# Later weight conversions in batch 0 and a filler that opens with two sums at once: one change to a fused attention and two-layer MLP kernel

## The chip, the cores and the metric

The kernel runs on one core of one Trainium2 chip. The metric is device time in microseconds, the median over runs; of each kernel one execution is also profiled.

## What is computed

Causal attention with a decay bias, then two MLPs of model width 512 and inner width 2048 over 2304 tokens, all in float32. Cut to what matters:

```python
scores = scale * q @ k.T                       # 4 batches, 8 heads, 576 tokens, head size 64
cum = cumsum(maximum(s, 0))
scores = where(causal, -1e9, scores + minimum(-(cum_i - cum_j), 0))
x = softmax(scores) @ v                        # heads side by side: 2304 x 512
h = x @ w_in;   x = (h * sigmoid(1.702 * h)) @ w_out
h = x @ w2_in;  g = P(h) / (Q(h) + 1e-6);  out = g @ w2_out
```

## The kernel before

**Precision.** Products run on TensorE (PE) from pairs of numbers: a float is split into a rounded high part and a low rest, and three products (high x high, low x high, high x low) make one. A block of weights is brought to that form by a **conversion** (`convert`, line 550): lines 558 and 560 on ScalarE (ACT), 561 to 563 on VectorE (DVE), 565 on GpSimd (POOL), 566 on ACT, 567 on POOL, each over 128 x 512 elements. Its raw block of 512 KB is loaded by SP's queue (`load_raw`, lines 547 and 549) into one of three slots of a staging tile, `stgA`. Ten conversions make the first MLP's inner blocks 0 to 4: five for `w_in`, then five for `w_out`. `emit` issues one; two raw loads are issued ahead of all.

**Attention.** A batch has four pairs of heads, a pair has five units: query blocks t = 0, 1, 4, 2, 3. There are 80 units, 20 in each batch. The loop of `attention` goes over steps j. Step j computes the scores of unit j on PE (line 289); DVE adds the mask and takes the minimum (line 319), ACT makes the exponential with its row sum (line 326), DVE the reciprocal (line 336), POOL the normalization (line 339). Three steps later PE transposes the unit (lines 360, 364, 381) and ACT or DVE copies the transposes out (lines 361, 365, 385, 388). A step after that PE multiplies with V (line 406, output `O`), and after t = 4 and t = 3 the values of the pair go to X: the high part by ACT (line 416), the low part by DVE (line 417). In batch 0 the values are taken as each unit is ready, later once per pair. In between, the next pair's Q and K are turned on PE (line 225) and split by ACT (line 213) and DVE (line 216), and moved to their places by POOL or SP.

**The filler.** From batch 1 on, the first MLP of the batch before is done beside the attention, by a generator, `mlp1_first`, that `fill` takes a piece of at three places of each step, by a credit of 1.65 us a step. First it makes ten sums of twelve products each (line 638, tiles `h`: inner blocks 0 to 4, two token halves), each followed by the activation (lines 649 and 652 on ACT, 650 on DVE, 655 on POOL), then the output blocks (line 662). It is started where unit i = j - 3 has i % 20 == 1, that is at steps 24, 44 and 64. Before step 24 PE has no filler; in the first five steps it runs dummy products.

**What sets the order.** PE's order is the program's. The other engines' order is made by a scheduler that keeps each engine's queue in one fixed order; `behind` (a block of `issue_after`) keeps instructions of a conversion from being placed ahead of a given instruction of the same engine. `CONV_J` lists the steps at whose end a conversion of the first ten is emitted, `AHEAD_J` (35 to 55) those of six more. PSUM has eight banks, which all tiles of this phase share.

Of the kernel before, what the change touches and what calls it, by code (L numbers as in the profile page):

```python
# [31 lines left out]
KD = DM // P  # L32
NF = DF // P
F1 = 5
HB = S // 2
# [16 lines left out]
RUN_ENDS = ((0, 1, 4, 2, 3), (3,), (3,), (3,))  # L52
W2_SLOTS = 7
LEAD = 2
CONV_J = (4, 6, 9, 12, 15, 18, 21, 24, 27, 30)
CONV = [(f, 0) for f in range(F1)] + [(f, 1) for f in range(F1)]
STG = 1536
BT_BUFS, G_BUFS = 9, 9
# [3 lines left out]
class Fused:  # L62
# [328 lines left out]
    def unit_values(self, att, u):  # L391
        nc = self.nc
        b, p, t = u
        pr, st = self.pairs[b, p], self.state.pop(u)
        vn = pr["ld"]["v"]
        R = min(P, S - t * P)
        NC = t + 1
        oc = {0: 0, 1: 128, 4: 256, 2: 0, 3: 128}[t]
        if b not in self.X:
            self.X[b] = self.xpool.tile([P, 2, KD, S], F32R, name=f"x{b}", tag="x", bufs=4)  # L400
        if oc == 0:
            pr["O"] = self.bank("O", f"O{b}_{p}_{t}")
        O = pr["O"]
        for c in range(NC):
            for h in range(2):
                nc.tensor.matmul(  # L406
                    O[64 * h : 64 * h + 64, oc : oc + R],
                    lhsT=vn[:, c, h, :], rhs=st["pt"][h, c],
                    start=(c == 0), stop=(c == NC - 1),
                )  # L410
        if t in (3, 4):
            X = self.X[b]
            runs = ((0, 256, 0), (256, 64, 512)) if t == 4 else ((0, 256, 256),)
            for o, w, x0 in runs:
                xh = X[:, 0, p, x0 : x0 + w]
                nc.scalar.activation(xh, O[:, o : o + w], AF.Copy)
                nc.vector.tensor_tensor(
                    X[:, 1, p, x0 : x0 + w], O[:, o : o + w], xh.bitcast(F32), ALU.subtract
                )

# [12 lines left out]
    def attention(self, att, mlp):  # L433
        units = [(b, p, t) for b in range(NB) for p in range(NP) for t in (0, 1, 4, 2, 3)]
        n = len(units)
        nc = self.nc
# [23 lines left out]
        opened = self.moved  # L460
# [3 lines left out]
        for j in range(n + AHEAD + 1):  # L464
            i, k = j - AHEAD, j - AHEAD - 1
            self.zeros = j < ZEROS
            tr = iter(())
            if j < n:
                b, p, t = units[j]
                idx = j % 5  # L470
                if idx == 0 and units[j][1:] != (NP - 1, 0) or (idx == 0 and b + 1 < NB):
                    nprep = self.prep(att, *divmod(b * NP + p + 1, NP), loads.pop(b * NP + p + 1))
            if i >= 0 and i < n and units[i][0] and i % 20 == 1:
                self.filler = chain(self.filler, self.mlp1_first(mlp, units[i][0] - 1))
                self.cold = False
            q = FILL / 20
            if j < n:
                self.unit_scores(att, units[j], 0)
                if j:
                    next(nprep, None)  # L480
                if j == 2:
                    with self.behind((opened,)):
                        later.pop(0)()
                    with self.behind((self.moved,)):
                        self.raw_ahead()
            self.fill(q / 3, 1 if j else 4)
            if 0 <= i < n:
                tr = self.unit_transpose(att, units[i])
                next(tr, None)
            if j < n:  # L490
                self.unit_scores(att, units[j], 1)
            self.fill(q / 3, j < 4)
            for _ in tr:
                pass
            if j < n and idx == 4:
                for _ in nprep:
                    pass
                g = b * NP + p
                g = {0: 3, 1: 4, 2: NB * NP}.get(g, g + 2)
                if g < NB * NP:  # L500
                    with self.behind((opened,)):
                        loads[g] = self.pair_load(att, *divmod(g, NP))
                    later.append(loads[g]["values"])
            if k >= 0:
                run.append(units[k])
                if units[k][2] in RUN_ENDS[units[k][0]]:
                    for u in run:
                        self.unit_values(att, u)
                    run.clear()
                if units[k][2] == 3 and later:  # L510
                    later.pop(0)()
            self.fill(q / 3, j < 4)
            if j == AHEAD_J[0]:
                self.stg_n, self.stg_k = 0, 2
                buf = self.stg_slot[:, 2 * STG : 2 * STG + 1024].bitcast(F32R)
                buf = buf.rearrange("p (i f) -> p i f", i=2)
                for f in AHEAD_F:
                    for half in range(2):
                        self.task(
                            lambda st, f=f, half=half: self.park(st, buf, 1, f, half), 1, f, half  # L520
                        )
            if j in COEF_J:
                with self.behind((*self.tail, self.moved)):
                    if j == COEF_J[0]:
                        self.coefficients()
                    else:
                        self.nc.scalar.activation(self.cf[:, 6:8], self.cf[:, 4:6], AF.Abs)
            if j in CONV_J or j in AHEAD_J:
                with self.behind((*self.tail, opened)):
                    self.emit(1)  # L530
        for _ in self.filler:
            pass
# [152 lines left out]
    def mlp1_first(self, pool, b):  # L685
        X = self.X[b]
        gs = [[], []]
        for f in range(F1):
            for hb in range(2):
                h = self.bank("h" if self.wide else "M", f"h{2 * b + hb}_{f}")  # L690
                x = lambda l, kk: X[:, l, kk, hb * HB : (hb + 1) * HB]
                yield from self.stage1(h[:, :HB], 1, f, x, 6)
                gs[hb].append(self.act1(pool, h[:, :HB], HB, G_BUFS))
                yield 0.74
        for hb in range(2):
            yield from self.out1_block(pool, 2 * b + hb, gs[hb])
# [313 lines left out]
```

## Time and profile before

| | us |
|---|---|
| median of 3 runs (lowest, highest) | 1022.4 (1020.93, 1025.38) |
| the profiled execution | 1021.61 |
| its span | 1019.6 |
| PE busy with matmuls, of the span | 998.2 (98%) |
| DVE, ACT, POOL busy | 797.3, 718.2, 337.8 |

The profiled execution is read as a timeline from the span's start; what lies around the span is 2.0 us. The mean granted clock of PE is 0.999 of its full 2.4 GHz. An engine's busy time is a sum over the span, so a stage that is limited by another engine than PE is seen in windows of that stage alone. Matmuls are pipelined, and the durations of neighbours overlap. Step 5 begins at 22 us, step 24 at 78 us, step 44 at 153 us; the attention's part of the trace is followed by the MLPs alone.

### The profile page before, as it was taken

The numbers are of one execution on the slowest core, as the hardware profiler recorded it, in microseconds if no ns is written. First come the engines' busy times: TensorE is split into PE (matmuls) and PEld (weight loads), VectorE is DVE, ScalarE is ACT, GpSimd is POOL, SyncE is SP. The second block draws the span as 40 slices with busy tenths as digits, with TensorE's granted clock in tenths as the row PEclk, the third lists the DMA queues.
The fourth block names the chain that finished last, engine by engine and source line by source line (L and its number), as shares of the span: only waits on it lengthen the run. The fifth ranks groups of instructions, "written<-read, shape, count | busy, mean of one in ns | idle before, by whom it ended". The sixth has DMA issues, their size and how long they took to land.

```text
span 1019.6 us, 19822 instructions
## 1 busy us (share of the span) xinstructions
PE 998.2 (98%) x7053; PEld 933.9 (92%) x7054; DVE 797.3 (78%) x1804; ACT 718.2 (70%) x1661; POOL 337.8 (33%) x503
## 2 busy tenths in 40 slices
PE   7889999999999999999999999999999999999997
PEld 4679999999999999999999999999999999989996
DVE  7897666766537977777778747998988989889886
ACT  5999889878756655555555436787887777777775
POOL 5778656554410012222111112232222222222222
PEclk9999999999999999999999999999999999999999
DMA  7664564543237546776666644010010100100000
GB/s 180 157 175 100 135 188 146 152 123 72 59 125 247 177 140 196 230 235 224 212 189 235 208 133 190 1 31 32 3 60 1 32 32 1 63 1 1 32 1 32
DMA packets 79074, 115.97 MB, mean 114 GB/s; under 512 B 25552, under 2 KB 63072, under 8 KB 77440
## 3 DMA queue, kind: packets, MB, share of 16 engines
q1 hardware_dynamic: 72640, 94.94, 31.4%
q0 software_dynamic: 6112, 19.47, 5.1%
q8 instruction: 56, 0.92, 0.4%
q14 instruction: 42, 0.34, 0.1%
q10 hardware_dynamic: 224, 0.30, 0.1%
HBM read 74.78 MB, written 31.60 MB: 104 GB/s over the span
## 4 chain that ended last, share of the span: by engine, by line
PE 89%; DVE 4%; DMA 3%; ACT 2%; issue 1%; POOL 0%; SPq 0%; ACTq 0%; DVEq 0%
PE h L638 38%; PE a L815 19%; PE a L662 19%; PE s L289 5%; PE O L406 4%; PE tp L381 3%; DMA raw<-in_moe_w_in_dram 1%; DVE bt L319 1%; DMA x2p<-st 1%; DVE k L216 1%; PE tq L225 1%; PE tk L225 1%; ACT bt L326 0%; PE tp L360 0%; DVE qs L216 0%
## 5 line engine op out<-in xcount | busy, mean ns | idle before, releaser
L638 PE MATMUL h<-x,u 128*128 128x288 f32 x1536 | 231.5, 296 | 1.2 <-ACT st L677 1.2
L662 PE MATMUL a<-gh,u 128*128 128x288 f32 x1024 | 231.7, 297 | 0.0
L638 PEld LDWEIGHTS h<-x,u 128*128 128x128 f32 x1536 | 212.8, 188 | 3.1 <-ACT st L677 1.5
L798 POOL TENSOR_TENSOR gl<-u,gh 128x384 fp32r<-128x384 f32 x96 | 105.7, 1101 | 290.4 <-ACT gh L796 266.4
L662 PEld LDWEIGHTS a<-gh,u 128*128 128x128 f32 x1024 | 173.0, 188 | 1.1 <-issue 0.5
L638 PE MATMUL h<-y,u 128*128 128x384 f32 x864 | 165.7, 336 | 0.0
L638 PEld LDWEIGHTS h<-y,u 128*128 128x128 f32 x864 | 152.9, 188 | 6.2
L662 PE MATMUL a<-gl,u 128*128 128x288 f32 x512 | 150.0, 295 | 0.7 <-DVE gl L655 0.7
L815 PE MATMUL a<-u,gh 128*128 128x512 f32 x432 | 114.6, 394 | 0.9 <-ACT gh L796 0.9
L649 ACT ACTIVATE g<-h 128x288 f32<-128x288 f32 x128 | 52.0, 407 | 75.8 <-PE h L638 75.4
L724 POOL DMA_DIRECT2D x<-xp x64 | 35.3, 552 | 207.3 <-DVE g L650 106.7
L662 PEld LDWEIGHTS a<-gl,u 128*128 128x128 f32 x512 | 96.5, 188 | 1.4 <-DVE gl L655 0.9
L326 ACT ACTIVATE bt<-bt,mn 128x128 f32<-128x128 f32 (+2 forms) x144 | 84.1, 585 | 19.3 <-DVE mn L319 18.2
L815 PEld LDWEIGHTS a<-u,gh 128*128 128x128 f32 x432 | 80.0, 188 | 14.9 <-ACT gh L796 1.8
L339 POOL TENSOR_SCALAR bt<-bt,sm 128x128 f32<-128x128 f32 (+2 forms) x144 | 81.7, 579 | 30.0 <-DVE sm L336 21.6
L796 ACT ACTIVATE gh<-u 128x384 fp32r<-128x384 f32 x96 | 50.6, 527 | 57.6 <-DVE u L794 56.6
L319 DVE CUSTOM_DVE_ANT_0 bt<-s,mask 128x128 f32<-128x128 f32 (+2 forms) x144 | 68.9, 482 | 27.6 <-PE s L289 25.5
L652 ACT ACTIVATE gh<-g 128x288 fp32r<-128x288 f32 x128 | 56.5, 442 | 45.6 <-DVE g L650 43.8
L650 DVE SCALAR_TENSOR_TENSOR g<-g,h 128x288 f32<-128x288 f32 x128 | 57.5, 450 | 29.8 <-ACT g L649 29.2
L781 ACT ACTIVATE y<-h,cf 128x384 f32<-128x384 f32 x96 | 55.4, 577 | 33.9 <-PE h L638 33.9
L786 DVE SCALAR_TENSOR_TENSOR y<-s,cf,y 128x384 f32<-128x384 f32 x96 | 59.3, 618 | 20.6 <-ACT s L783 19.3
L794 DVE SCALAR_TENSOR_TENSOR u<-y,u 128x384 f32<-128x384 f32 x96 | 73.5, 765 | 1.1
(116 smaller groups left out, 2048.0 us busy)
## 6 DMA issues: line engine op xcount, KB each, us to landing
raw<-in_moe_w_in_dram SPq DMA_DIRECT2D x24, 512.0 KB
raw<-in_moe_w_out_dram SPq DMA_DIRECT2D x24, 512.0 KB
x<-xp POOLq DMA_DIRECT2D x64, 144.0 KB, 3.0
wd<-park POOLq DMA_DIRECT2D x36, 256.0 KB, 4.3
u<-wd SPq DMA_DIRECT2D x8, 1024.0 KB
x2p<-st SPq DMA_DIRECT2D x32, 144.0 KB
xp<-x2p SPq DMA_DIRECT2D x32, 144.0 KB
xp<-x SPq DMA_DIRECT2D x32, 144.0 KB
```

The lines of the kernel that those rows point to most:

```text
L319: nc.vector.tensor_tensor_reduce(bt[:, j0 : j0 + w], sc[:, :w], mask, 1.0, 3.0e38 if i == 0 else mn[:, 0:1], ALU.add, ALU.min, mn[:, i : i ...
L326: ex = nc.scalar.activation(bt[:, :n], bt[:, :n], AF.Exp, bias=mn[:, i : i + 1], scale=-1.0, accum_out=sm[:, col : col + 1],)
L339: nc.gpsimd.tensor_scalar(bt[:, :n], bt[:, :n], inv[:, i : i + 1], 1.0, ALU.mult, ALU.mult)
L638: nc.tensor.matmul(ps_tile, lhsT=u[:, wl, kk * P : (kk + 1) * P], rhs=x(xl, kk), start=(n == 0), stop=(n == 3 * KD - 1),)
L650: nc.vector.scalar_tensor_tensor(g[:, :w], g[:, :w], 1.0, h, ALU.add, ALU.mult)
L652: self.newest["act"] = nc.scalar.activation(gh[:, :w], g[:, :w], AF.Copy)
L662: nc.tensor.matmul(acc, lhsT=u[:, wl, d * P : (d + 1) * P], rhs=g[gl], start=(first and i == 0), stop=(last and i == 2),)
L781: nc.scalar.activation(y, h, AF.Abs, scale=cf[:, 4:5])
L786: nc.vector.scalar_tensor_tensor(y, s, cf[:, 7:8], y, ALU.mult, ALU.add)
L794: last = nc.vector.scalar_tensor_tensor(p, y, 2.0, p, ALU.subtract, ALU.mult)
L798: nc.gpsimd.tensor_tensor(gl, p, gh.bitcast(F32), ALU.subtract)
L815: nc.tensor.matmul(accs[m], lhsT=g[gl][:, m * P : (m + 1) * P], rhs=u[:, wl, :], start=(f == 0 and i == 0), stop=(f == NF - 1 and i == 2),)
```

## The change

The first ten conversions are emitted at steps 7, 11, 15, 18, 20, 23, 25, 27, 29, 31 in place of 4, 6, 9, 12, 15, 18, 21, 24, 27, 30. The one at step 23 is also placed behind DVE's last write of X (`kept`). The filler of batch 0 starts at i = 20, step 23; those of batches 1 and 2 start where they did. For batch 0 the filler opens with both token halves of inner block 0 at once: nine products of the first sum and nine of the second, which read pairs 0 to 2 of X, then the last three products of each, which read pair 3, whose values are computed at step 23. The other eight sums follow as before.

```diff
@@ -52,7 +52,7 @@
 RUN_ENDS = ((0, 1, 4, 2, 3), (3,), (3,), (3,))
 W2_SLOTS = 7
 LEAD = 2
-CONV_J = (4, 6, 9, 12, 15, 18, 21, 24, 27, 30)
+CONV_J = (7, 11, 15, 18, 20, 23, 25, 27, 29, 31)
 CONV = [(f, 0) for f in range(F1)] + [(f, 1) for f in range(F1)]
 STG = 1536
 BT_BUFS, G_BUFS = 9, 9
@@ -414,7 +414,7 @@
             for o, w, x0 in runs:
                 xh = X[:, 0, p, x0 : x0 + w]
                 nc.scalar.activation(xh, O[:, o : o + w], AF.Copy)
-                nc.vector.tensor_tensor(
+                self.kept = nc.vector.tensor_tensor(
                     X[:, 1, p, x0 : x0 + w], O[:, o : o + w], xh.bitcast(F32), ALU.subtract
                 )
 
@@ -470,7 +470,7 @@
                 idx = j % 5
                 if idx == 0 and units[j][1:] != (NP - 1, 0) or (idx == 0 and b + 1 < NB):
                     nprep = self.prep(att, *divmod(b * NP + p + 1, NP), loads.pop(b * NP + p + 1))
-            if i >= 0 and i < n and units[i][0] and i % 20 == 1:
+            if i in (20, 41, 61):
                 self.filler = chain(self.filler, self.mlp1_first(mlp, units[i][0] - 1))
                 self.cold = False
             q = FILL / 20
@@ -526,7 +526,8 @@
                     else:
                         self.nc.scalar.activation(self.cf[:, 6:8], self.cf[:, 4:6], AF.Abs)
             if j in CONV_J or j in AHEAD_J:
-                with self.behind((*self.tail, opened)):
+                tail = (*self.tail, self.kept) if j == 23 else self.tail
+                with self.behind((*tail, opened)):
                     self.emit(1)
         for _ in self.filler:
             pass
@@ -685,7 +686,22 @@
     def mlp1_first(self, pool, b):
         X = self.X[b]
         gs = [[], []]
-        for f in range(F1):
+        open2 = int(b == 0)
+        if open2:
+            parts = []
+            for hb in range(2):
+                h = self.bank("M", f"h{hb}_0")[:, :HB]
+                x = lambda l, kk, hb=hb: X[:, l, kk, hb * HB : (hb + 1) * HB]
+                parts.append((h, self.stage1(h, 1, 0, x, 3)))
+            for _, part in parts:
+                for _ in range(KD - 1):
+                    yield next(part)
+            for hb, (h, part) in enumerate(parts):
+                for _ in part:
+                    pass
+                gs[hb].append(self.act1(pool, h, HB, G_BUFS))
+                yield 0.37
+        for f in range(open2, F1):
             for hb in range(2):
                 h = self.bank("h" if self.wide else "M", f"h{2 * b + hb}_{f}")
                 x = lambda l, kk: X[:, l, kk, hb * HB : (hb + 1) * HB]
```

Beside this, lines move: up to line 528 they stay, then by one, and from `mlp1_first` on by sixteen.

The first place is ACT's queue about step 23, from the exponential of unit 22 on. Names read `bt_pair_t`; `x` written from `O_3_2` is the copy of pair 3's last values. Before:

```order
L326 ACTIVATE bt_0_4_0_1231,sm_0_4_1230<-bt_0_4_0_1231,mn_0_4_0_1232 128x576
L416 ACTIVATE x_78<-O_3_0_1104 128x64
L326 ACTIVATE bt_0_2_0_1270,sm_0_2_1269<-bt_0_2_0_1270,mn_0_2_0_1271 128x384
L388 COPY pt_0_0_1277<-tp_0_0_0_1278 128x256
L326 ACTIVATE bt_0_2_1_1282,sm_0_2_1269<-bt_0_2_1_1282,mn_0_2_1_1283 128x384
L416 ACTIVATE x_78<-O_3_2_1262 128x256
L326 ACTIVATE bt_0_3_0_1307,sm_0_3_1306<-bt_0_3_0_1307,mn_0_3_0_1308 128x512
L388 COPY pt_0_1_1321<-tp_0_1_0_1322 128x512
L566 ACTIVATE u_1_508<-stgA 128x512
L649 ACTIVATE g<-h_0_1314 128x288
```

With the change:

```order
L326 ACTIVATE bt_0_2_0_1252,sm_0_2_1251<-bt_0_2_0_1252,mn_0_2_0_1253 128x384
L567 ACTIVATE u_4_1142<-stgA 128x512
L326 ACTIVATE bt_0_2_1_1272,sm_0_2_1251<-bt_0_2_1_1272,mn_0_2_1_1273 128x384
L559 ACTIVATE stgA<-stgA 128x512
L561 ACTIVATE stgA<-stgA 128x512
L416 ACTIVATE x_78<-O_3_2_1244 128x256
L326 ACTIVATE bt_0_3_0_1315,sm_0_3_1314<-bt_0_3_0_1315,mn_0_3_0_1316 128x512
L388 COPY pt_0_1_1325<-tp_0_1_0_1326 128x512
L650 ACTIVATE g<-h_0_1259 128x288
L650 ACTIVATE g<-h_0_1260 128x288
```

Lines 559 and 561 are 558 and 560 of before. Ahead of the exponential of `bt_0_2_0`, unit 23's first, stand seven such pairs and six conversions' third instructions (566) before, and five and four (567) with the change; the sixth pair now stands ahead of the copy of `O_3_2`.

The second place is PE's queue from unit 23's second scores on. `h_0` and `h_1` are sums of the filler for inner blocks 0 and 1. Before:

```order
L289 MATMUL s_0_2_1_1284<-k_0_134 128x384
L289 MATMUL s_0_2_1_1284<-kh_0_873,qs_0_874 128x384
L406 MATMUL O_3_2_1262<-pt_3_3_1239,vn_118 64x128 x8
L289 MATMUL s_0_3_0_1309<-k_0_134 128x512
L289 MATMUL s_0_3_0_1309<-kh_0_873,qs_0_874 128x512
L638 MATMUL h_0_1314<-x_78,u_0_385 128x288 x6
L381 MATMUL tp_0_1_0_1322<-ident,bt_0_1_0_1161 128x128 x2
L381 MATMUL tp_0_1_0_1322<-ident,bt_0_1_1_1191 128x128 x2
L289 MATMUL s_0_3_1_1330<-k_0_134 128x512
L289 MATMUL s_0_3_1_1330<-kh_0_873,qs_0_874 128x512
L638 MATMUL h_0_1314<-x_78,u_0_385 128x288 x6
L638 MATMUL h_0_1356<-x_78,u_0_385 128x288 x6
```

With the change, from the end of the same step:

```order
L639 MATMUL h_0_1259<-x_78,u_0_538 128x288 x3
L406 MATMUL O_3_2_1244<-pt_3_3_1221,vn_118 64x128 x8
L639 MATMUL h_0_1260<-x_78,u_0_538 128x288 x6
L289 MATMUL s_0_3_0_1317<-k_0_134 128x512
L289 MATMUL s_0_3_0_1317<-kh_0_853,qs_0_854 128x512
L639 MATMUL h_0_1260<-x_78,u_0_538 128x288 x3
L381 MATMUL tp_0_1_0_1326<-ident,bt_0_1_0_1152 128x128 x2
L381 MATMUL tp_0_1_0_1326<-ident,bt_0_1_1_1182 128x128 x2
L289 MATMUL s_0_3_1_1334<-k_0_134 128x512
L289 MATMUL s_0_3_1_1334<-kh_0_853,qs_0_854 128x512
L639 MATMUL h_0_1259<-x_78,u_0_538 128x288 x3
L639 MATMUL h_0_1260<-x_78,u_0_538 128x288 x3
```

Ahead of this piece six products of `h_0` now stand between the first scores and the transposes of step 23. The last products of both opening sums, six in all, stand behind the scores `s_0_3_1`.

The third place is POOL's queue in batch 1, between the normalizations of unit 27 (`bt_1_4_0`) and of unit 28 (`bt_1_2_0`). `gl` belongs to the filler, `stgA` and `u` to conversions. Before:

```order
L339 TENSOR_SCALAR bt_1_4_0_1509<-bt_1_4_0_1509,sm_1_4_1508 128x576
L335 TENSOR_SCALAR sm_1_2_1569<-sm_1_2_1569 128x2
L655 TENSOR_TENSOR gl<-g,gh 128x288
L565 TENSOR_TENSOR stgA<-stgA 128x512
L339 TENSOR_SCALAR bt_1_2_0_1570<-bt_1_2_0_1570,sm_1_2_1569 128x384
L339 TENSOR_SCALAR bt_1_2_1_1595<-bt_1_2_1_1595,sm_1_2_1569 128x384
L655 TENSOR_TENSOR gl<-g,gh 128x288
```

With the change:

```order
L339 TENSOR_SCALAR bt_1_4_0_1520<-bt_1_4_0_1520,sm_1_4_1519 128x576
L656 TENSOR_TENSOR gl<-g,gh 128x288
L568 TENSOR_TENSOR u_1_731<-stgA,u_1_731 128x512
L566 TENSOR_TENSOR stgA<-stgA 128x512
L335 TENSOR_SCALAR sm_1_2_1593<-sm_1_2_1593 128x2
L656 TENSOR_TENSOR gl<-g,gh 128x288
L568 TENSOR_TENSOR u_2_899<-stgA,u_2_899 128x512
L339 TENSOR_SCALAR bt_1_2_0_1594<-bt_1_2_0_1594,sm_1_2_1593 128x384
L339 TENSOR_SCALAR bt_1_2_1_1606<-bt_1_2_1_1606,sm_1_2_1593 128x384
```

One more `gl` and two more of the conversions' second instructions (567, now 568) stand ahead of unit 28's normalization.

## Rows read from the trace of the kernel before

**Rows 1.** Windows by stage: us, busy us (instructions) of PE, PEld, DVE, ACT, POOL, clock, DMA share.

```profile
...
22.00:78.50 56.50, 49.57 (x478) 38.66 (x475) 51.29 (x179) 55.40 (x158) 41.54 (x66) 1.00 0.66 171
78.50:120.00 41.50, 40.77 (x388) 39.17 (x387) 30.56 (x99) 37.10 (x108) 33.05 (x49) 1.00 0.45 116
120.00:165.00 45.00, 44.06 (x421) 42.52 (x420) 30.15 (x104) 39.50 (x114) 24.61 (x42) 1.00 0.63 176
...
300.00:1020.00 720.00, 711.95 (x4354) 672.88 (x4353) 590.22 (x1110) 470.32 (x957) 160.81 (x196) 1.00 0.32 107
```

**Rows 2.** PE's waits, 22 to 78.5 us: engine, line, releaser: us in total, times, longest.

```profile
PE tp L360 <- POOL bt L339: 2.2, 3, 0.9
PE tp L381 <- DVE mn L319: 2.1, 3, 1.2
PE tq L225 <- DVE pt L361: 1.1, 1, 1.1
PE tp L381 <- POOL bt L339: 1.0, 2, 0.6
...
```

**Rows 3.** PE's waits, 78.5 to 165 us.

```profile
PE tq L225 <- ACT pt L361: 0.9, 1, 0.9
PE tq L225 <- DVE mn L319: 0.5, 1, 0.5
...
```

**Rows 4.** The conversions' tile, 22 to 78.5 us: duration ns min/median/max, first and last start.

```profile
...
L558 ACT ACTIVATE stgA<-stgA x7: 657/675/702, 24.9 to 74.7; 128x512 int32<-128x512 uint32 x7
L560 ACT ACTIVATE stgA<-stgA x7: 662/672/681, 25.4 to 75.2; 128x512 f32<-128x512 f32 x7
L561 DVE TENSOR_SCALAR stgA<-stgA x7: 404/426/767, 26.1 to 76.5; 128x512 f32<-128x512 f32 x7
L562 DVE TENSOR_SCALAR stgA<-stgA x7: 417/645/800, 27.1 to 77.4; 128x512 int32<-128x512 int32 x7
L563 DVE SCALAR_TENSOR_TENSOR stgA<-stgA x7: 670/681/693, 28.2 to 78.1; 128x512 int32<-128x512 int32 x7
...
L566 ACT ACTIVATE u<-stgA x6: 610/628/670, 31.0 to 73.4; 128x512 fp32r<-128x512 f32 x6
L567 POOL TENSOR_TENSOR u<-stgA,u x6: 1287/1291/1789, 31.7 to 74.1; 128x512 fp32r<-128x512 f32 x6
...
```

**Rows 5.** Timeline of ACT, first conversions: start us, us, engine, line, operation, out<-in.

```profile
...
24.86 0.66 ACT L558 ACTIVATE stgA<-stgA 128x512 int32<-128x512 uint32 x1
25.42 0.66 ACT L560 ACTIVATE stgA<-stgA 128x512 f32<-128x512 f32 x1
...
38.98 0.61 ACT L566 ACTIVATE u<-stgA 128x512 fp32r<-128x512 f32 x1
39.49 0.87 ACT L213 ACTIVATE kh<-tk 64x288 fp32r<-64x288 f32 x2
...
```

**Rows 6.** Timeline of PE, where the filler begins, and one transpose of batch 1.

```profile
...
76.78 1.23 PE L406 MATMUL O<-pt,vn 128*64 128x128 f32 x16
...
78.52 0.96 PE L638 MATMUL h<-x,u 128*128 128x288 f32 x6
...
80.23 1.75 PE L638 MATMUL h<-x,u 128*128 128x288 f32 x12
...
107.09 0.49 PE L381 MATMUL tp<-ident,bt 128*128 128x128 f32 x3
...
```

**Rows 7.** Timeline of ACT, the copy of pair 3's values into X.

```profile
...
79.08 0.41 ACT L416 ACTIVATE x<-O 128x256 fp32r<-128x256 f32 x1
...
```

**Rows 8.** Timeline of POOL: a long subtraction; unit 28's normalization and the filler's subtraction behind it.

```profile
...
59.46 1.79 POOL L567 TENSOR_TENSOR u<-stgA,u 128x512 fp32r<-128x512 f32 x1
...
99.98 1.15 POOL L339 TENSOR_SCALAR bt<-bt,sm 128x384 f32<-128x384 f32 x2
101.09 0.82 POOL L655 TENSOR_TENSOR gl<-g,gh 128x288 fp32r<-128x288 f32 x1
...
```

**Rows 9.** Timeline of DVE at that long subtraction.

```profile
...
59.42 0.69 DVE L563 SCALAR_TENSOR_TENSOR stgA<-stgA 128x512 int32<-128x512 int32 x1
...
```

## The prediction

> **What bounds the kernel now.** I read the windows of the stages first, because the page's 98% for PE is an average over stages [rows 1]. From 22 to 78.5 us, units 5 to 24 of the attention with no filler, PE's matmuls are busy 49.57 of 56.5 us, so 6.93 us are idle; ACT is busy 55.40 us, DVE 51.29, POOL 41.54. From 78.5 us the filler runs beside the attention and PE idles 0.73 us up to 120 us and 0.94 us up to 165 us. The last 720 us idle 8.05 us and are not touched. So what the change can win lies in the first 165 us, 8.60 us in all, and nearly all of it in batch 0. A microsecond won there is won at the end, since PE is full behind it.
>
> The list of PE's waits says who ends the idle time [rows 2]: POOL's normalization of a softmax block, DVE's masked minimum, DVE's copy of a transpose. None of the three is the real limit; all of them stand in chains through ACT's exponential, and ACT is the engine with no room. Its rows follow each other without a gap over most of the stretch: it idles 1.1 us in 56.5.
>
> **The cost of a conversion** [rows 4, 5]. On ACT, lines 558, 560 and 566: from the start of 558 to the start of 560 are 0.56 us, I take the same for 560 (672 ns against 675), and 0.51 us from the start of 566 to the next instruction: 1.63 us of the queue. On DVE 0.43 + 0.65 + 0.68 = 1.75 us, on POOL 1.29 us for line 567, and I take the same for 565, which has the same shape: 2.6 us. Nothing of a conversion is on PE.
>
> **Term 1, the conversions moved.** When ACT reaches the exponential of unit 23's first scores, it has done seven pairs of 558 and 560 and six 566 before the change, five and four with it. That is 2 x 1.63 = 3.3 us less in a queue that has 1.1 us of idle time. PE's floor is not in the way (3.3 of 6.93 us), DVE and POOL lose 3.5 and 5 us. I take -3.3 us. Ends: 0, if latency alone sets the pace; -6.93, the whole idle time of the stretch. The value lies with ACT's own rows because ACT is the fullest engine.
>
> **Term 2, unit 23.** The sixth conversion is emitted there, and 15 products of the filler run a unit sooner. Six products take 0.96 us and twelve 1.75, so one is 0.13 us and 15 are 2.0 us of PE's time [rows 6]. ACT's 1.63 us go beside them: zero. The products are not new work, they leave the filler's later part.
>
> **Term 3, the last pair's products.** They wait for X of pair 3, and PE's queue waits behind them. The values of pair 3 ended at 76.78 + 1.23 = 78.01 us [rows 6], ACT's copy of them started at 79.08 us and took 0.41 [rows 7], that is 1.5 us after the values. The new pair of ACT instructions stands ahead of that copy: 1.5 + 1.12 = 2.6 us. On PE the same way to the last pair's products was 80.23 - 78.01 = 2.22 us, with six products in it; now nine, so 2.6 us. The second product needs DVE's half too, some 0.4 us more. I take +0.2 us; ends 0 and +0.9 (the longest wait of PE in this region [rows 3]). The hold of the conversion behind DVE's write of X keeps DVE from making that longer.
>
> **Term 4, units 24 to 34.** At unit 24's first exponential only one conversion of the two is still outstanding, and it is made up by unit 31: ACT gets 1.6 us more here, and it idled 41.5 - 37.1 = 4.4 us in this window [rows 1]. PE is covered by the filler as long as ACT stays within its room; its waits up to 120 us are 0.73 us already. I take +0.2 us; ends -0.7 (both go) and +1.6 (as long as the extra work itself).
>
> **Term 5, before the second filler.** The first filler starts a unit sooner and ends sooner, the second is still appended at unit 44, so PE has one unit more without filler. In batch 0 ACT without its conversions needed 55.4 - 7 x 1.12 - 6 x 0.51 = 44.5 us where PE was busy 49.6, so ACT can keep up through such a unit. I take +0.1 us; ends -0.9 (the 0.9 us wait behind this place goes [rows 3]) and +0.9 (it doubles).
>
> **DMA.** The raw loads move with their conversions on SP's queue, behind the rows of the sums and a pair's move of Q or K. The one for unit 23 has the least lead, from about unit 20's K move, some 7 us; 512 KB at the window's 171 GB/s [rows 1] are 3.1 us. Zero; what hides it is that lead.
>
> **Sum.** -3.3 + 0.2 + 0.2 + 0.1 = -2.8 us against the profiled execution of 1021.6 us: 1018.8 us. The median of the runs shown, 1022.4, lies 0.8 us above that execution. The 0.5% that a measurement of this kernel can tell from no change are 5.1 us, so "faster" begins below 1017.3 us.
>
> **Rivals.**
> - *A, the chains shorten too.* Beside ACT's 3.3 us, its 1.1 us of idle time and the waits of 0.9 and 0.5 us go [rows 1, 3], since DVE and POOL lose more work than ACT and the conversion no longer sits between a transpose and its copy. Ahead of units 5 to 7 the waits of 1.1 us for DVE's copy and part of the 2.1 us for the minimum [rows 2] stand right behind the first conversion, which speaks for it; ACT's fullness speaks against it. 3.3 + 1.1 + 1.4 = 5.8 us at most, with half of what goes beyond 3.3 some 4.6: 1015.8 to 1017.3, about 1017.0. Chance 0.24.
> - *B, the order doesn't matter.* The conversions only fill gaps of in-order queues, and the waits reappear at the new places (units 7, 11, 20). PE keeps 5.5 to 6.9 us of idle time in the stretch: 0 to 1.4 us won, 1021 us. Against it: two conversions really leave the stretch. Chance 0.16.
> - *C, POOL is late in batch 1: slower.* Between the normalizations of unit 27 and of unit 28, POOL now has two more finishing subtractions of conversions and one more of the filler's, 2 x 1.29 + 0.82 = 3.4 us [rows 4, 8]. In the trace that normalization ended at 99.98 + 1.15 = 101.1 us, and PE took its block at 107.09 us [rows 6]: 6.0 us of room. It decides once POOL is 2.6 us later still. Then PE stands with the filler behind it, for up to 3 us, and again a unit or two on: +5 in all, less the 3.3: 1023 us. One subtraction took 1.79 us where the others took 1.29, with DVE's two-input instruction of 0.69 us inside it [rows 8, 9], so such lateness exists. Chance 0.08, of which 0.03 beyond 0.5%.
>
> The Trainium skill speaks for C: "SBUF — State Buffer", section "Who interferes with whom", says that VectorE's instructions with two SBUF inputs, or in a two-port mode, and GpSimd's block each other for a whole instruction. By that rule, three more POOL instructions can each be held for one of DVE's 0.68 us: 3.4 + 2.0 = 5.4 us against the room of 6.0, still inside it, and C's time would then be reached with 0.6 us more. The trace agrees in one POOL instruction of six; DVE's two one-input instructions spread from 404 to 800 ns.
>
> **How the numbers follow.** My forecast has 0.52, with its own range of 1017.3 to 1020.6 (terms 3 to 5 between their nearer ends); A 0.24, B 0.16, C 0.08. The range of 1015.2 to 1022.2 takes in A and B and leaves out C and the tails. Faster by over 0.5% is A and a lower tail of the forecast: 0.26. Slower by over 0.5% is C's far end: 0.03. The rest, 0.71, is within 0.5%.
>
> **What would show it.** Right: in the windows the stretch up to the first scores of unit 24 is some 3 us shorter, ACT still full in it and PE idle there 3 to 4 us; the filler's first products start about 6 us earlier in the trace (a unit and the gain); the wait at the last pair's products is under 0.9 us; PE idle up to 120 us at most 1.5 us. Term 1 is wrong if ACT shows idle time in batch 0 while PE's idle time stays over 5 us. A shows as PE idle under 2.5 us there, C as waits of a transpose for POOL's normalization between 85 and 110 us. The prediction is wrong as a whole if the time changes by more than these stretches do, since nothing behind 165 us should move.

## The result, and the profile after

The changed kernel took 1033.4 us (median of 6 runs, 1030.9 to 1034.8), the kernel before in the same series 1022.3 (6 runs, 1020.9 to 1025.4): 1.0101 times as long, 95% interval 1.0086 to 1.0116. The medians lie 11.1 us apart; the ratio stands for 10.3 us (8.8 to 11.9). 1018.8 had been forecast, with a range up to 1022.2. The profiled execution of the change is one of the long ones: 1034.8 us, span 1032.9. The profile shows where PE stood still or ran slower; the comparison of times goes by the medians.

The windows of [rows 1], now of the change (busy us and instructions of PE, PEld, DVE, ACT, POOL; clock; DMA share; GB/s):

```profile
22.00:78.50 56.50, 52.26 (x498) 41.43 (x497) 50.63 (x177) 54.18 (x154) 35.98 (x63) 1.00 0.60 151
78.50:120.00 41.50, 35.65 (x295) 33.55 (x294) 30.19 (x92) 36.61 (x102) 33.13 (x48) 0.96 0.48 122
120.00:165.00 45.00, 42.62 (x414) 40.47 (x416) 25.48 (x85) 31.42 (x88) 19.73 (x34) 0.92 0.52 144
```

Batch 0 got denser: PE is busy 52.3 us of the first window where it was 49.6; that takes in the filler's first products, which run in this window only now. The loss stands in the next two. PE idles 5.85 and 2.38 us there, 8.23 in all, where it idled 0.73 and 0.94; that is 6.6 us more. And the granted clock, 1.00 before, is 0.96 and 0.92.

The same stretch in short windows:

```profile
111.00:114.00 3.00, 3.00 (x15) 2.98 (x15) 2.70 (x8) 2.98 (x10) 1.77 (x5) 0.50 0.51 148
121.40:127.80 6.40, 5.85 (x21) 5.33 (x21) 1.59 (x5) 1.69 (x5) 1.32 (x2) 0.51 0.36 105
```

In 3.0 us from 111 us and 5.85 busy us from 121.4 PE ran at 1.2 GHz, half its clock, which cost about half of each, 1.5 + 2.9 = 4.4 us. With the 6.6 us of idle time that makes 11.0. It is an estimate of the loss in these two windows, which don't hold exactly the same work before and after. A landmark measures better: 60 products of O that started at 170.96 us before start at 182.32 now, 11.36 us later, and every following one up to 294.95 us (306.31 now) is later by the same amount. The windows up to this landmark, before and with the change, hold nearly the same work (1410 and 1411 products by their counts):

```profile
0.00:170.96 170.96, 157.25 (x1410) 136.24 (x1412) 133.71 (x442) 149.52 (x421) 116.88 (x195) 1.00 0.59 156
0.00:182.32 182.32, 165.37 (x1411) 142.72 (x1412) 135.38 (x441) 150.07 (x421) 115.09 (x195) 0.95 0.56 146
```

PE idles 17.0 us where it idled 13.7, and is busy 8.1 us longer with the same products: 3.2 + 8.1 = 11.4 us. So 11.0 and 11.36 come out alike in part by luck. The landmark also holds what batch 0 won, and a stretch at half clock from 11.5 to 18.4 us, by which this execution entered unit 5 1.2 us late.

"Nothing behind 165 us should move" held only up to 306 us. The span is 13.3 us longer, so 1.9 us more were lost behind the last of these landmarks: after waits of 0.9 and 0.7 us, close together, PE ran at half clock from 329.0 to 332.4 us. The profile of experiment 4 has such a stretch too (at 342 us), the twelve others have none there; no run shows whether it belongs to the change.

PE's waits of [rows 3], from 78.5 to 165 us, in the change (us in total, times, longest):

```profile
PE a L663 <- ACT u L567: 4.2, 1, 4.2
PE h L639 <- DVE mn L319: 1.9, 1, 1.9
...
PE a L663 <- POOL u L568: 0.5, 1, 0.5
```

The largest is of a kind that the list of before does not have: line 663 is the filler's output block, and `u` a block of w_out that the last conversion has not finished. PE's timeline there (start, us, instruction, count, idle time before it and releaser):

```profile
108.60 1.06 PE L639 MATMUL h<-x,u 128*128 128x288 f32 x6 [1.88 <-DVE mn L319]
...
116.53 0.29 PE L663 MATMUL a<-gh,u 128*128 128x288 f32 x1
116.67 0.60 PE L381 MATMUL tp<-ident,bt 128*128 128x128 f32 x4
121.44 0.61 PE L663 MATMUL a<-gh,u 128*128 128x288 f32 x1 [4.18 <-ACT u L567]
121.85 0.44 PE L663 MATMUL a<-gl,u 128*128 128x288 f32 x1
122.80 0.61 PE L663 MATMUL a<-gh,u 128*128 128x288 f32 x1 [0.51 <-POOL u L568]
```

The product at 116.53 took 0.29 us, the one at 121.85, of the same shape and behind the wait, 0.44: the clock fell while PE stood. The Trainium skill ("TensorE: Matmul & The Clock Gate", section "HAM oscillation — how this bites in real kernels") has this pattern: a wait re-throttles the array and the next work starts cold. These rows agree with it.

The smaller wait, 1.9 us at 108.60, is for a PSUM bank that is free when DVE has taken a minimum. DVE's timeline ahead of it:

```profile
106.88 0.17 DVE L336 RECIPROCAL sm<-sm 128x2 f32<-128x2 f32 x1 [1.47 <-POOL sm L335]
...
107.41 0.80 DVE L563 TENSOR_SCALAR stgA<-stgA 128x512 int32<-128x512 int32 x1
108.13 0.41 DVE L319 CUSTOM_DVE_ANT_0 bt<-s,mask 128x256 f32<-128x256 f32 x1
```

DVE stood 1.5 us for POOL's line 335 (the row sums of the softmax, ahead of their reciprocal), and the minimum stood behind that and behind two instructions of a conversion.

The conversion that PE waited for, the tenth, stands on three in-order queues. Its part of ACT's timeline:

```profile
113.67 0.67 ACT L559 ACTIVATE stgA<-stgA 128x512 int32<-128x512 uint32 x1
114.53 0.67 ACT L561 ACTIVATE stgA<-stgA 128x512 f32<-128x512 f32 x1
...
120.76 0.63 ACT L567 ACTIVATE u<-stgA 128x512 fp32r<-128x512 f32 x1 [2.79 <-POOL stgA L566]
```

Of DVE's:

```profile
116.96 0.41 DVE L562 TENSOR_SCALAR stgA<-stgA 128x512 f32<-128x512 f32 x1
117.40 0.43 DVE L563 TENSOR_SCALAR stgA<-stgA 128x512 int32<-128x512 int32 x1
117.86 0.85 DVE L564 SCALAR_TENSOR_TENSOR stgA<-stgA 128x512 int32<-128x512 int32 x1
```

And of POOL's, with the softmax's instructions between:

```profile
117.51 1.55 POOL L339 TENSOR_SCALAR bt<-bt,sm 128x256 f32<-128x256 f32 x2 [1.79 <-DVE stgA L562]
...
119.45 1.28 POOL L566 TENSOR_TENSOR stgA<-stgA 128x512 int32<-128x512 int32 x1
...
121.47 1.27 POOL L568 TENSOR_TENSOR u<-stgA,u 128x512 fp32r<-128x512 f32 x1
```

From its first instruction to its last it took 9.1 us (113.67 to 122.74), of which its own instructions are some 6.2. The rest it stood behind the softmax and the filler's activation in the queues: DVE's first instruction began 1.8 us after ACT's second had ended, POOL's first 0.7 us after DVE's last. It can't be taken as 1.6 us of ACT when the question is when it is *done*.

In the kernel before, the same conversion ended in time, but not by much. POOL's last instruction of it in POOL's timeline of before:

```profile
115.25 1.28 POOL L567 TENSOR_TENSOR u<-stgA,u 128x512 fp32r<-128x512 f32 x1
```

And the third of the products that use this block first, in PE's timeline of before:

```profile
118.27 0.29 PE L662 MATMUL a<-gh,u 128*128 128x288 f32 x1
```

It reads what POOL wrote; it started at 118.27, POOL was done at 116.53. The room was 1.7 us. The change emits the conversion a step later (31 for 30) and needs it a step sooner (the filler opens at step 23 for 24), and a step takes 4.0 us here (two pairs' first K transposes at 82.06 and 122.01 us, ten steps apart). So by this estimate the room went from +1.7 to about -6.3 us; PE waited 4.7. (The expectations below were written with a step of 3.3 us and a conversion of 8 us; the rows give 4.0 and 9.1.)

### The profile page after: what moved, and what is told of

Same layout as the page of the kernel before. It is cut to its first block, busy times and chain, and to the rows that moved or that the text cites. A ratio compares the mean times of both kernels' runs of the same rounds, so it can differ in the third digit from the quotient of the medians.

```text
span 1032.9 us, 19816 instructions
## 1 busy us (share of the span) xinstructions
PE 1008.1 (98%) x7053; PEld 941.9 (91%) x7054; DVE 800.1 (77%) x1804; ACT 719.5 (70%) x1661; POOL 336.6 (33%) x503
## 4 chain that ended last, share of the span: by engine, by line
PE 86%; DVE 4%; ACT 4%; POOL 2%; issue 1%; DMA 1%; SPq 0%; ACTq 0%; POOLq 0%; DVEq 0%
PE h L639 36%; PE a L663 20%; PE a L831 19%; PE s L289 4%; PE O L406 3%; PE tp L381 2%; ACT bt L326 1%; DMA raw<-in_moe_w_out_dram 1%; DVE bt L319 1%; POOL bt L339 1%; POOL u L568 1%; DVE qs L216 1%; PE tk L225 1%; PE tq L225 0%; ACT qs L213 0%
## 5 line engine op out<-in xcount | busy, mean ns | idle before, releaser
L663 PE MATMUL a<-gh,u 128*128 128x288 f32 x1024 | 235.6, 301 | 5.6 <-ACT u L567 4.2
L663 PEld LDWEIGHTS a<-gh,u 128*128 128x128 f32 x1024 | 176.0, 191 | 7.6 <-ACT u L567 4.4
L289 PE MATMUL s<-k 68*128 68x256 f32 (+2 forms) x192 | 72.7, 383 | 2.8 <-DMA k<-stgA 1.5
```

Of the source, the lines that this page charges most:

```text
L289: nc.tensor.matmul(sc[: c1 - c0, :w], lhsT=q[:, c0:c1], rhs=k[:, j0 : j0 + w], start=m == 0, stop=m == 1,)
L663: nc.tensor.matmul(acc, lhsT=u[:, wl, d * P : (d + 1) * P], rhs=g[gl], start=(first and i == 0), stop=(last and i == 2),)
```

## The experiments

Theory **T**: the last conversion comes too late for the output block, PE waits, and the clock falls behind the wait. Rival **R1**: the conversions, packed into steps 20 to 31, make DVE and POOL late wherever the last one is due. Rival **R2**: the filler's new opening costs by itself. Ratios are to the kernel before, run on the same chip. *Lead* is the number of steps between the end of the step that emits the last conversion and the third of a step in which the order of PE's queue has its first product: 2.67 before, 0.67 in the change.

**1. The old list, the new filler.** Lead 1.67.

```diff
-CONV_J = (7, 11, 15, 18, 20, 23, 25, 27, 29, 31)
+CONV_J = (4, 6, 9, 12, 15, 18, 21, 24, 27, 30)
```

> The changed kernel with the list of conversions put back (4, 6, 9, ... 30); the filler still opens a step sooner with its two sums together. Theory T (the last conversion of w_out comes too late for the filler's output block: it is emitted at the end of step 31, its products are due in the last third of step 32, and it took 8 us from its first instruction to its last): now it is emitted at the end of step 30, a step of some 3.3 us sooner, so of the 4.2 + 0.5 us that PE waited about 1 us is left and the stretch at the half clock behind it goes; early in batch 0 the 1.7 us won are lost again. 1021 to 1025 us. Rival R1 (seven conversions packed into steps 20 to 31 keep POOL and DVE late, wherever the last one is due): here they are spread as before, so 1021 to 1023 us as well. Rival R2 (the filler's opening, sooner and two sums at once, is itself what costs): the loss stays, 1030 to 1034 us.

Measured: 1027.9 us, ratio 1.0043 (1.0028 to 1.0058), between T's and R2's figures. PE's timeline there:

```profile
115.48 0.40 PE L663 MATMUL a<-gh,u 128*128 128x288 f32 x1 [0.49 <-ACT u L567]
117.94 0.49 PE L663 MATMUL a<-gh,u 128*128 128x288 f32 x1 [1.93 <-POOL u L568]
```

And a window behind it, with the columns of the windows above:

```profile
118.00:123.00 5.00, 5.00 (x31) 4.83 (x33) 1.75 (x6) 1.79 (x5) 0.95 (x2) 0.66 0.09 30
```

The wait is T's, 2.4 us where the room of 1.7 less a step of 4.0 gives 2.3; I had expected 1. And the clock (0.66 in the window) fell behind this wait too, which I had not expected.

**2. The new list, the old filler and opening.** Lead 1.67, packed as in the change. (The edit of experiment 1 the other way, in the kernel before.)

> The kernel before with the new list of conversions alone; the filler opens as before, so its output block needs the last conversion in the last third of step 33, 1.67 steps behind its emission and not 0.67. Theory T: the wait of 4.7 us shrinks by a step of some 3.3 us to 1 to 2 us, the clock stays up; with 1.7 us won in batch 0 the time is 1020 to 1025 us. R1: the conversions are packed as in the change, so most of the loss stays, 1028 to 1034 us. R2: without the sooner opening nothing is lost, 1019 to 1021 us, with no wait of the output block at all.

Measured: 1024.4 us, ratio 1.0013 (1.0003 to 1.0023): T's range. The wait of the output block is 0.7 us, the clock is 1.00 throughout. So the packing alone is not the 11 us. It is not free either: what batch 0 won is gone, and PE's waits are short ones, of 0.9 us at most: for ACT's copy of a transpose (as before), DVE's part of the activation, the conversion and the minimum.

**3. The last two conversions sooner.** Lead 2.67, packed more.

```diff
-CONV_J = (7, 11, 15, 18, 20, 23, 25, 27, 29, 31)
+CONV_J = (7, 11, 15, 18, 20, 23, 25, 27, 28, 29)
```

> The changed kernel with the last two conversions at steps 28 and 29 for 29 and 31: later still denser (27, 28, 29). The last one now has 2.67 steps, some 9 us, ahead of the products that need it, as in the kernel before. Theory T: no wait at the output block and no half clock behind it: 7 to 10 us are won back, 1021 to 1026 us (the waits for DVE's minimum may grow, since three conversions follow each other in three steps). R1: the packing is worse, so the time stays at 1031 to 1037 us, with longer waits between 95 and 110 us.

Measured: 1025.7 us, ratio 1.0024 (1.0014 to 1.0034). Two numbers give back 7.7 of the 11 us, while the packing got worse. Of the output block's wait 0.4 us are left; R1 has its part in the other row of PE's timeline:

```profile
110.38 1.49 PE L639 MATMUL h<-x,u 128*128 128x288 f32 x6 [2.74 <-DVE mn L319]
118.88 0.40 PE L663 MATMUL a<-gh,u 128*128 128x288 f32 x1 [0.40 <-POOL u L568]
```

PE's bank is free when DVE has taken the minimum: 2.7 us of waiting where the change had 1.9. DVE's timeline ahead of it:

```profile
108.37 0.17 DVE L336 RECIPROCAL sm<-sm 128x2 f32<-128x2 f32 x1 [1.26 <-POOL sm L335]
108.45 1.53 DVE L562 TENSOR_SCALAR stgA<-stgA 128x512 f32<-128x512 f32 x1
109.90 0.41 DVE L319 CUSTOM_DVE_ANT_0 bt<-s,mask 128x256 f32<-128x256 f32 x1
```

DVE waited for POOL again, and then one instruction of a conversion took 1.53 us, where this one took 0.43 in median before [rows 4]. PE's clock fell behind this wait as well (0.50 from 110.8 to 114.2 us).

**4. Products of zeros in place of the wait.** The values of the output tile whose bank they share are changed by them; the kernel's own products and their order are the same.

```diff
+                if blk == 0 and d == 0 and f == F1 - 1:
+                    for _ in range(48):
+                        nc.tensor.matmul(
+                            acc[:, HB:], lhsT=self.idle[:, :P], rhs=self.idle[:, : 512 - HB],
...
                 self.out1(acc[:, :HB], self.units[1, f], d, gs[f], f == 0, f == F1 - 1)
```

> The changed kernel with 48 products of zeros (128x128 by 128x224, bf16) on PE ahead of the first product of the filler's output block that waits for the last conversion. They write columns of the bank that the block does not use, and fill the 4.2 us that PE stands there. Theory T with the clock as a part of its price: the products behind the wait run at the full clock, which took 5.85 us for some 21 products at half rate in the change, so 2.5 to 3 us are won back: 1030 to 1031 us, and the granted clock of that stretch is near 1. Rival R3 (the clock costs nothing by itself, only the wait counts, or the half clock has another cause): 1033 to 1034 us and the half clock stays.

Measured: 1031.8 us, ratio 1.0081 (1.0062 to 1.0100). That lies between T's and R3's figures. By the medians 1.6 us are won, and the intervals overlap; the trace tells more. PE's timeline:

```profile
116.22 4.76 PE L675 MATMUL a<-mask 128*128 128x224 bf16 x48
120.75 0.38 PE L663 MATMUL a<-gh,u 128*128 128x288 f32 x1
...
121.90 0.40 PE L663 MATMUL a<-gh,u 128*128 128x288 f32 x1 [0.64 <-POOL u L568]
...
124.75 1.46 PE L406 MATMUL O<-pt,vn 128*64 128x128 f32 x32
```

Its window behind the wait:

```profile
122.00:126.00 4.00, 4.00 (x51) 3.84 (x53) 1.66 (x6) 1.68 (x5) 0.21 (x1) 1.00 0.32 119
```

PE was kept busy until the conversion came, and the clock behind it is 1.00. From the awaited product to the 60 products of O (the row at 124.75) are 4.0 us here; in the change 6.4 (121.44 to 127.81) for the same work. So the clock cost 2.4 us here, and it fell because PE stood. Beyond 0.6 us the wait itself is only filled, not gone.

**5. The filler a unit later, as before; the rest of the change as it is.**

```diff
-            if i in (20, 41, 61):
+            if i in (21, 41, 61):
```

> The changed kernel with the filler opened at unit 21 as before; the two sums that run together, the new list of conversions and the hold stay. It differs from the kernel with the new list alone by the paired opening and the hold. Theory T (the last conversion's due time decides, with PE's clock behind the wait): its products now come 1.67 steps behind the last conversion and not 0.67, so the wait at the output block is under 1 us, as it was in the kernel with the new list alone (0.7 us), and the time is 1021 to 1025 us. Rival R2 (the opening with two sums together costs by itself): 1028 us or more, with waits of the filler's products for the minimum or for X between 75 and 115 us.

Measured: 1023.7 us, ratio 1.0010 (1.0001 to 1.0019). Theory T's range; the output block waits 1.0 us for POOL. This one number is worth 9.7 us to the changed kernel. R2 falls as far as the paired opening goes.

**6. The kernel before, the last conversion alone moved.** Lead 0.67, no packing.

```diff
-CONV_J = (4, 6, 9, 12, 15, 18, 21, 24, 27, 30)
+CONV_J = (4, 6, 9, 12, 15, 18, 21, 24, 27, 32)
```

> The kernel before with one number changed: the last conversion at step 32 for 30, the other nine where they were, the filler as before. Its lead over the products that need it falls from 2.67 steps to 0.67, as in the change, with no packing of the others. Theory T: PE waits 3 to 5 us for that conversion (ACT's copy, then POOL's subtraction), and the clock falls to half behind it; 4.7 us and up to 3 us: 1026 to 1031 us. Rival R1 (packing, not the due time): one conversion two steps later costs nothing, 1022 to 1024 us, no wait of the output block over 1 us.

Measured: 1027.4 us, ratio 1.0040 (1.0026 to 1.0054). PE's timeline:

```profile
120.37 0.40 PE L662 MATMUL a<-gh,u 128*128 128x288 f32 x1 [0.86 <-ACT u L566]
122.06 0.41 PE L662 MATMUL a<-gh,u 128*128 128x288 f32 x1 [1.16 <-POOL u L567]
```

And the window behind it:

```profile
122.00:126.00 4.00, 3.94 (x15) 3.67 (x16) 1.16 (x3) 1.16 (x3) 0.00 (x1) 0.57 0.55 159
```

The due time costs by itself, and the clock falls with it, here in a kernel that has nothing else of the change. The waits are 2.0 us and not 3 to 5, for two reasons of about the same size. This conversion took 7.6 us from its first to its last instruction (114.45 to 122.01), where the change's took 9.1; that the packing made the difference isn't shown. And steps aren't equally long: here 60 products of O stand ahead of the awaited product,

```profile
116.52 2.99 PE L406 MATMUL O<-pt,vn 128*64 128x128 f32 x60
```

so that PE came to it 5.1 us after the conversion's first instruction, in the change after 3.6.

**7. and 8. Everything done in time, two steps apart.** Both have a lead of 2.67, experiment 7 in the kernel before, experiment 8 in the change.

```diff
+CONV_J = (7, 11, 15, 18, 20, 22, 24, 26, 28, 30)
```

```diff
+CONV_J = (7, 11, 14, 16, 18, 20, 22, 24, 27, 29)
```

> The kernel before with the list (7, 11, 15, 18, 20, 22, 24, 26, 28, 30): two conversions still leave batch 0, the rest stand two steps apart, and the last is where it was; the filler as before. Theory T: the 1.6 to 2.7 us won in batch 0 stay, the output block has its 2.67 steps, so nothing is paid but small waits: 1020 to 1022 us, at or just under the kernel before. R1: a conversion every two steps is already too dense for DVE and POOL: waits for the minimum of 1 to 3 us between 85 and 115 us, 1024 to 1028 us.

> The changed kernel, opening and hold included, with the list (7, 11, 14, 16, 18, 20, 22, 24, 27, 29): every conversion from the third on is sooner than in the change, two steps apart and more, the last 2.67 steps ahead of its products. Theory T: no wait at the output block and none of the clock; one conversion less leaves batch 0, 1 us won there: 1020 to 1023 us. R1: if a conversion every two steps makes DVE and POOL late the wait for DVE's minimum of 1.9 us at step 31 stays or moves: 1025 to 1029 us.

Measured: 1024.9 us, ratio 1.0018 (1.0010 to 1.0027), and 1028.3, ratio 1.0051 (1.0039 to 1.0063). Both miss T's figures and fall in R1's, and the output block is in neither list of waits. R1's sign, waits of 1 us and more for the minimum, shows in experiment 8 alone. The largest are others; PE's waits of experiment 8 from 76 to 165 us:

```profile
PE h L639 <- DVE x L417: 2.3, 2, 1.8
PE h L639 <- DVE mn L319: 1.3, 1, 1.3
```

The first is X of the last pair, late by 1.8 us in both kernels, which alone of all have a conversion at step 22. DVE's timeline in experiment 7:

```profile
79.45 0.85 DVE L562 TENSOR_SCALAR stgA<-stgA 128x512 int32<-128x512 int32 x1
80.22 0.67 DVE L319 CUSTOM_DVE_ANT_0 bt<-s,mask 128x512 f32<-128x512 f32 x1
...
80.82 1.15 DVE L563 SCALAR_TENSOR_TENSOR stgA<-stgA 128x512 int32<-128x512 int32 x1
81.89 0.41 DVE L417 TENSOR_TENSOR x<-O,x 128x256 fp32r<-128x256 f32 x1
```

The conversion's two instructions stand ahead of line 417, whose result PE waits for with the filler behind it. The change holds its conversion at step 23 behind just this instruction; at step 22 there is no such hold. So by these rows a conversion costs by the place where it stands, not only by its neighbours; no run has the conversion at step 22 held.

**9. A milder list.** Filler at unit 21, one conversion out of batch 0, lead 2.67.

```diff
+CONV_J = (5, 8, 11, 14, 17, 20, 23, 25, 28, 30)
```

> The changed kernel with the filler opened at unit 21 as before and the list (5, 8, 11, 14, 17, 20, 23, 25, 28, 30): one conversion leaves batch 0 instead of two, none stands at step 22 (where it made X of the last pair late by 1.8 us in two kernels), and the last is where it was before, 2.67 steps ahead of its products. Theory T, with the measured prices: 1.3 us won in batch 0, waits for conversions and for the minimum under 0.5 us each: 1021 to 1023 us, at or 1 us under the kernel before. Rival R1 (two conversions two and three steps apart behind step 23 are dense enough to be late): 1024 to 1026 us.

Measured: 1023.2 us, ratio 1.0005 (0.9996 to 1.0014): no difference that can be told, and just over T's range. The waits for the minimum are 0.9 and 0.8 us, where T had asked for under 0.5; with them the gain in batch 0 is gone.

**10. One number of experiment 1.** Lead 2.67 again, filler a unit sooner.

```diff
-CONV_J = (4, 6, 9, 12, 15, 18, 21, 24, 27, 30)
+CONV_J = (4, 6, 9, 12, 15, 18, 21, 24, 27, 29)
```

> The changed kernel with the list of before but for its last number, 29 for 30: (4, 6, 9, ... 27, 29). It differs by that number from the kernel with the old list and the sooner filler (1027.9 us), where PE waited 0.5 + 1.9 us for the last conversion with the clock falling behind it; the last one has 2.67 steps again. Theory T: that wait and the half clock go, 3 to 4 us: 1023.5 to 1025 us. Rival: what the sooner filler costs is something else than this due time (the load on ACT, DVE and POOL of a filler that starts a unit sooner): 1027 to 1029 us.

Measured: 1023.5 us, ratio 1.0007 (0.9997 to 1.0017). 4.4 us come back for one conversion one step sooner, and PE waits nowhere for the output block. Clear of noise, the sooner filler costs nothing but the due time that it brings forward.

**11. The paired opening alone.** Old list, filler at unit 21.

> The changed kernel with the list of conversions and the filler's unit both put back: of the change only the two sums that run together are left. Rival R2 would have them cost by themselves. With the kernel that had the new list and this opening at 1.001 times before, theory T says they cost and win next to nothing: 1022 to 1024 us. If the paired opening is worth its wait, up to 1 us is won (1021 to 1022 us).

Measured: 1022.5 us, ratio 1.0002 (0.9991 to 1.0012). R2 falls; the opening wins nothing either.

**12. The filler a unit later than before, the rest of the change as it is.** Lead 2.67.

```diff
-            if i in (20, 41, 61):
+            if i in (22, 41, 61):
```

> The changed kernel with one number put the other way: the filler opened at unit 22, a unit later than before and two later than in the change; list, opening and hold as in the change. The last conversion again has 2.67 steps ahead of its products. Theory T: no wait at the output block, the 1.6 to 2.7 us won in batch 0 stay, and one or two units without filler cost PE up to 1 us of idle time each: 1021 to 1024 us. Rival R1 (the packing of the list costs at any place of the filler): 1025 us or more.

Measured: 1021.5 us, ratio 0.9991 (0.9982 to 0.9999), the only ratio whose interval lies under 1, if by little. Its windows:

```profile
78.50:120.00 41.50, 39.58 (x372) 37.30 (x371) 32.41 (x101) 39.05 (x111) 35.78 (x52) 1.00 0.52 137
120.00:165.00 45.00, 44.78 (x427) 43.24 (x426) 30.71 (x104) 38.36 (x112) 24.39 (x42) 1.00 0.62 171
```

PE idles 1.92 and 0.22 us where the change idled 5.85 and 2.38, and the clock is 1.00 in both. Same list, same opening, same hold: only the filler's unit differs. Medians by that unit: 1033.4 at 20, 1023.7 at 21, 1021.5 at 22.

## Why the prediction was wrong, point by point

**Term 1 (-3.3 us): the gain is there, its size is -2.5.** Experiment 12 shows it best, since its profile enters unit 5 where the one before does (first K transpose at 22.37 against 22.41 us) and has no filler ahead of the next landmark: the 16 products of O that started at 76.78 us [rows 6] start at 74.22. From 22 us to the filler's place PE still idles 4.3 us there, and ACT is busy 52.0 of 53.9 us: it idles 1.9 us where it idled 1.1. So ACT is still nearly full, and PE's idle time stands in waits. That the gain came from ACT's queue, and not from DVE's or POOL's, which lost work too, is argued and not shown. Two of the waits, in the change's list from 22 to 78.5 us, with the first in a place where before had none of that length:

```profile
PE tp L381 <- DVE k L216: 1.4, 1, 1.4
PE O L406 <- ACT pt L385: 0.9, 1, 0.9
```

The lower end of the term had allowed for that. The profiled execution of the change shows less: its 16 products start at 76.66, but nine of the filler's products now stand ahead of them, and it ran at half clock from 11.5 to 18.4 us and entered unit 5 1.2 us late. Such stretches, 3 to 7 us long about 12 or 30 us, stand in nine of the fourteen profiles, with the old list too (experiment 6 at 30 us, 11 at 12 us), and not in that of experiment 4, whose program is the change's up to there; so they are no effect of the change.

**Term 2 (0)** is supported: the paired opening alone is 1.0002. **Term 3 (+0.2)** came out at nothing: in the change PE's list of waits from 78.5 to 165 us has none for X. (A wait of 0.4 us for X stands at 168.63, where the second filler opens.)

**Term 4 (+0.2, ends -0.7 and +1.6) is the step that failed.** It asked whether ACT had room for one more conversion ("ACT gets 1.6 us more here, and it idled 4.4 us in this window") and not when the last one is *due*. The 1.6 us were right as load and meaningless as a bound: the end of this conversion has a reader on the engine that sets the time, and the two parts of the change moved writer and reader toward each other by a step each. The rows for it were in the trace of before: POOL done at 116.53, read at 118.27, 1.7 us of room against two steps of 4.0 us. In the runs: a lead of 2.67 steps cost no wait of the block over 0.4 us (experiments 3, 7, 8, 9, 10, 12), 1.67 steps 0.7 to 2.4 us (1, 2, 5), 0.67 steps 2.0 (6) to 4.7 us (the change). The room counted in steps gives the sign and not the size: 1.7 less one step of 4.0 is -2.3 us, and the waits were 2.4, 0.7 and 1.0; less two it is -6.3, and they were 2.0 and 4.7. I also took a wait at its length; behind this one the clock added 2.4 us (experiment 4), and by the windows 1.5 more behind the wait for the minimum.

**Term 5 (+0.1) and DMA (0)** show no loss: from 78.5 to 165 us PE waits for no load. The wait of 0.9 us behind the second filler's opening [rows 3] is gone, and one of 0.4 us for X came at the opening.

**Rival C** named a real piece, but not the way it costs. POOL was late: it ended unit 28's normalization at 105.8 us, 101.1 before. But no transpose waited for it, which was C's sign. POOL's line 335 behind it held DVE, and the minimum behind that held PE's bank: 1.9 us at 108.60, and 2.7 in experiment 3. As the main cause it falls: experiments 2 and 5 have the same packing at 1.0013 and 1.0010, experiment 10 the sooner filler at 1.0007, and experiment 3 both, and denser, at 1.0024. **Rivals A and B** had no part in the loss. I had a slower case at 0.03, with the wrong mechanism: none of my rivals asked for a due time.

How the 11 us split is shown in part only. The last conversion's due time is 7.7 us by experiment 3, which packs more, and 9.7 by experiment 5, which also changes the load beside it. Part of the rest is the wait for the minimum with its own half clock. I ran no kernel with that wait alone taken away.

## What to carry to other kernels

For each piece of work that a change moves, find who reads its last result, and compare the two times in the trace; then count how many steps each side moves, since two harmless moves toward each other add up. The count says whether the reader will wait; how long it waits came out up to 4.3 us shorter here. Price a wait of PE with the clock behind it. And if work is taken off one place, look for what stands ahead of the most awaited instruction in the place it goes to.

## What the runs showed that I had not expected

PE's clock fell to half after waits of 1.8 to 1.9 us with a short one beside them (at 108.60 in the change, with 0.6 us behind it; 1.9 us in experiment 1, with 0.5 us shortly before it; 1.8 us in experiment 7, with 0.2 us before it), and after two of middle length close together (0.9 and 1.2 us in experiment 6, 0.9 and 0.7 us about 328 us in the change). It stayed there for 3 to 6.4 us of work. It didn't fall after single waits of 1.0 us in experiments 5 and 12, of 1.2 us in 5 and of 1.5 us in 1 and 10. Nor did it in experiment 8 after a wait as long as experiment 7's and for the same instruction, with no short one beside it (PE's timeline, then a window with the columns of the windows above; the clock is 1.00):

```profile
84.92 1.73 PE L639 MATMUL h<-x,u 128*128 128x288 f32 x11 [1.83 <-DVE x L417]
84.00:87.00 3.00, 2.08 (x17) 2.08 (x18) 2.08 (x8) 2.44 (x7) 1.57 (x3) 1.00 0.30 47
```

So in these runs the length of the longest wait alone doesn't decide it. The clock also fell near the start in profiles whose waits there were like those of the kernel before, which kept its clock: the same program can show the fall in one execution and not in the next. In the last series eight executions of the kernel before have a mean clock of 0.999 and took 1021.3 us on average, 26 of the other 27 have 0.995 to 0.998 and took 1023.2.
